# A second-stage DFT table without its zeros, spread onto zeroed memory, in a new sequence

## The chip, the cores and the metric

The kernel runs on one core of a Trainium2 chip. The metric is the device time of one execution in microseconds (us). The engines are called TensorE (PE in the profile, PEld its weight loads), VectorE (DVE), ScalarE (ACT), GpSimd (POOL) and SyncE (SP, which issues most DMAs).

## The reference

There are four residual layers on x of shape [2048, 512]: A, B, A, B. Layer A is an H3-style mixer: k is convolved with four taps for each channel, multiplied by v, convolved over the whole sequence with a kernel of length 2048 for each channel (through an FFT of length 4096), and gated with the normalised x. Layer B is an MLP of width 1376.

```python
def _A_ref(q, k, v, shift_k, ssm_k, ssm_D):
    ...
    for t in range(ks):                       # ks = 4
        k_shift = k_shift + k_pad[:, t:t + S, :] * shift_k[:, ks - 1 - t][None, None, :]
    kv = k_shift * v
    ...
    y_f = kv_f * kf_f[None, :, :, :]          # rfft of kv and of ssm_k, both padded to 2S
    y = irfft(y_f)[:S]                        # shortened here
    y = y + kv * ssm_D[None, None, :]
    return q * y

def _B_ref(x, w1, b1, w2, b2):
    y = _layernorm(x, axis=-1)
    h = _gelu(jnp.einsum("bsd,df->bsf", y, w1) + b1)
    return jnp.einsum("bsf,fd->bsd", h, w2) + b2

x = A_q
x = x + _A_ref(_layernorm(x, axis=-1), A_k, A_v, A_shift_k, A_ssm_k, A_ssm_D)
x = x + _B_ref(_layernorm(x, axis=-1), B_w1, B_b1, B_w2, B_b2)
x = x + _A_ref(...)                           # the same k, v and taps again
x = x + _B_ref(...)
```

The convolution is the same in both A layers, since k, v and the kernel are the same; the kernel computes it once.

## The kernel before

The whole program is recorded as 1114 operations (`P.op`), each with the engines that may run it, the memory it reads and writes, and its PSUM tile. Nothing is planned at run time: the tuple `ORDER` lists the operations' numbers in the order in which they are handed to their engines, `SECOND` names those that go to the second of two allowed engines, and `BANKS` gives each PSUM tile its bank. Every engine runs its own operations strictly in that order, and waits on semaphores where an operation needs another engine's result (`sync`). DMAs are operations of SP's queue (a few of ScalarE's).

The FFT is done as matrix products with tables. The names in the code (line numbers of the profile):

- `ht` (L528, evacuated at L453): TensorE transposes ssm_k with the identity, in four tiles of 16 matmuls; the identity comes from `tab_small` by ScalarE's first DMA.
- `h1` (L545): the first stage of the kernel's transform, 16 tiles of 16 matmuls with 64 weight columns.
- `h2` (L558, `stage2`): its second stage, 128 matmuls, one for each of 128 frequencies, in 16 tiles of eight; the weight of each is a 128x128 block of the table S2, which lies in `R_S2`. Then 16 DMAs (ar<-ar, 512-byte runs) make a copy with swapped partitions.
- `fir`: the four-tap filter, for two channel groups on VectorE (L450, 128x2048) and for two on TensorE (L589 transposes, L606 products, L613 multiplication by v). GpSimd makes the diagonal matrices for it (L520).
- `x1` (L545) and `x2` (L651, `products`): the two stages for kv; the second again takes the 128 blocks of S2 as weights, for 64 columns at a time, 256 matmuls in 16 tiles of 16. An evacuation by ScalarE or VectorE (L453) is followed by a VectorE multiplication with the kernel's spectrum (L450).
- `i1` (L674) and `i2` (L731): the inverse, 256 matmuls of 128 columns and 64 of 256 columns; the weights of `i1` are read at a step of four elements.
- Then, block by block of rows (`BLOCKS0`, `BLOCKS1`): statistics (L754, L756, L760, L762), norm (L768), gate and add (L450), a transposition (TensorE at L814 for the first two rows of blocks, DMA at L807 for the others), the first product `m1` (L827), gelu on ScalarE (L832), the second product `m2` (L860; L849 for the last), and the residual addition (L864, L853).

S2 holds, for each frequency, a 128x128 matrix that couples 32 rows and 32 columns for one of four channels d, so that three quarters of it are zeros: a row (r, a, d) meets only columns with the same d. Before, the whole table of 128 x 16384 bf16 lies in DRAM and is loaded by 16 DMAs of 1024 columns (L447), which in SP's queue stand between the loads of v. The loads of k, v and the table are recorded by `load(step)` in the order of `LOADS`; that gives them their numbers (before: 10 to 19 for k, 20 to 27 for v, 28 to 43 for the table).

One operation is number 4 in both kernels: `P.op(ACT, lambda e: e.preload_act_table(AF.Gelu_apprx_tanh))` (L465). It has no input, no output and no successor.

Of the kernel before, what the change touches and what calls it, by code (L numbers as in the profile page):

```python
# [38 lines left out]
class Prog:  # L39
# [6 lines left out]
        49, 0, 47, 8, 7, 1, 3, 6, 48, 14, 71, 68, 5, 72, 18, 17, 15, 12, 4, 69, 9, 70, 50, 16, 65, 13, 19, 94, 2, 53, 73, 96, 51, 52, 11,  # L46
        92, 66, 305, 62, 95, 100, 97, 67, 104, 93, 63, 28, 64, 90, 88, 105, 10, 101, 26, 44, 45, 84, 91, 24, 56, 78, 85, 79, 86, 33, 59, 76,
        89, 57, 87, 198, 77, 36, 102, 168, 60, 103, 35, 25, 98, 30, 27, 31, 82, 74, 310, 182, 54, 169, 80, 61, 29, 183, 58, 199, 99, 37, 22,
        154, 75, 46, 81, 83, 172, 184, 42, 32, 155, 43, 120, 110, 116, 173, 121, 111, 34, 55, 112, 113, 39, 124, 158, 200, 125, 185, 20,
        106, 201, 108, 117, 23, 114, 107, 21, 38, 41, 159, 118, 109, 128, 156, 115, 136, 119, 122, 202, 40, 186, 203, 129, 157, 141, 204,  # L50
        132, 137, 133, 123, 134, 166, 170, 167, 187, 205, 130, 162, 171, 306, 144, 135, 126, 131, 127, 164, 138, 174, 163, 206, 175, 165,
        176, 207, 178, 139, 180, 140, 212, 179, 181, 160, 177, 188, 142, 213, 210, 295, 146, 208, 153, 209, 161, 189, 150, 211, 214, 148,
        223, 215, 224, 217, 147, 218, 151, 220, 192, 196, 193, 145, 194, 221, 149, 190, 197, 195, 235, 143, 225, 219, 226, 191, 236, 297,
        222, 304, 152, 229, 232, 230, 298, 296, 257, 216, 299, 227, 254, 237, 231, 233, 263, 228, 258, 264, 260, 234, 255, 269, 275, 259,
        252, 261, 303, 270, 253, 242, 294, 250, 243, 256, 265, 276, 262, 271, 246, 266, 272, 376, 277, 267, 300, 268, 248, 273, 274, 247,
        238, 249, 239, 333, 421, 240, 377, 334, 244, 251, 284, 241, 245, 477, 285, 311, 335, 288, 479, 289, 278, 313, 419, 336, 337, 314,
        338, 279, 378, 420, 286, 379, 287, 292, 380, 422, 290, 280, 339, 531, 293, 282, 342, 423, 478, 291, 529, 315, 281, 424, 283, 425,
        480, 302, 581, 316, 307, 381, 321, 323, 430, 331, 324, 325, 317, 322, 481, 329, 382, 340, 301, 326, 383, 341, 332, 308, 431, 482,
        343, 384, 426, 344, 385, 345, 386, 530, 346, 387, 347, 319, 388, 318, 432, 389, 330, 428, 348, 483, 349, 320, 390, 327, 354, 427,
        532, 391, 438, 328, 392, 368, 352, 533, 356, 309, 350, 355, 429, 364, 435, 433, 409, 360, 486, 357, 351, 358, 434, 353, 365, 436,  # L60
        439, 437, 362, 484, 363, 440, 485, 393, 487, 361, 394, 441, 397, 372, 410, 582, 395, 398, 366, 401, 489, 403, 442, 370, 359, 396,
        402, 534, 404, 367, 413, 407, 399, 443, 445, 538, 405, 411, 373, 583, 488, 635, 406, 400, 408, 312, 535, 491, 369, 490, 584, 371,
        492, 444, 414, 633, 415, 374, 416, 493, 446, 634, 494, 636, 497, 585, 586, 453, 536, 412, 454, 495, 590, 539, 451, 459, 637, 638,
        537, 465, 447, 591, 455, 466, 375, 461, 452, 540, 739, 449, 587, 642, 541, 592, 457, 498, 460, 450, 417, 448, 463, 496, 588, 643,
        543, 418, 462, 464, 507, 458, 509, 456, 542, 737, 685, 467, 589, 639, 503, 505, 499, 506, 544, 504, 515, 508, 469, 640, 468, 510,
        470, 593, 513, 687, 511, 473, 517, 545, 686, 738, 644, 740, 519, 546, 688, 689, 512, 549, 471, 550, 501, 690, 595, 516, 594, 596,
        547, 597, 502, 474, 514, 789, 548, 500, 641, 791, 598, 691, 694, 475, 525, 692, 521, 695, 551, 561, 518, 520, 567, 522, 476, 693,
        526, 599, 555, 645, 553, 696, 741, 742, 601, 552, 565, 527, 795, 554, 472, 646, 563, 566, 602, 743, 697, 562, 569, 557, 793, 746,
        571, 647, 699, 790, 600, 523, 568, 558, 570, 556, 524, 621, 648, 649, 572, 792, 744, 794, 559, 796, 698, 603, 560, 747, 611, 564,
        650, 651, 573, 609, 797, 607, 612, 700, 701, 748, 745, 605, 606, 652, 798, 653, 619, 528, 869, 608, 623, 620, 577, 615, 617, 802,  # L70
        702, 624, 799, 800, 613, 803, 574, 801, 749, 705, 654, 610, 706, 618, 614, 808, 751, 578, 703, 673, 669, 604, 575, 670, 576, 665,
        579, 622, 659, 667, 657, 750, 811, 616, 666, 809, 625, 871, 626, 661, 674, 675, 873, 870, 752, 872, 580, 753, 804, 660, 810, 662,
        754, 875, 874, 629, 876, 704, 805, 711, 658, 676, 806, 655, 725, 712, 663, 627, 812, 630, 817, 877, 878, 631, 709, 656, 668, 757,
        628, 888, 726, 671, 672, 758, 889, 813, 715, 681, 807, 716, 815, 885, 719, 755, 949, 723, 879, 664, 717, 724, 707, 632, 882, 682,
        886, 677, 756, 720, 816, 713, 883, 814, 880, 818, 881, 819, 683, 773, 951, 890, 678, 710, 820, 823, 684, 825, 827, 721, 950, 727,
        887, 759, 679, 884, 891, 892, 714, 761, 708, 824, 729, 821, 826, 718, 897, 762, 774, 769, 767, 680, 952, 728, 763, 895, 760, 896,
        953, 771, 779, 722, 730, 898, 775, 955, 822, 893, 770, 954, 765, 894, 956, 957, 733, 768, 958, 962, 828, 780, 777, 965, 899, 900,
        901, 731, 905, 734, 766, 968, 735, 764, 903, 839, 966, 963, 902, 785, 907, 831, 840, 776, 964, 732, 959, 906, 969, 781, 736, 960,
        778, 772, 845, 782, 973, 904, 908, 835, 843, 786, 787, 841, 1031, 967, 788, 929, 1029, 913, 846, 961, 970, 783, 784, 975, 1033,
        1035, 842, 844, 1030, 930, 836, 925, 976, 1032, 971, 911, 1034, 829, 849, 1036, 1037, 1038, 915, 912, 909, 972, 830, 923, 1045, 977,  # L80
        833, 832, 919, 974, 1046, 926, 978, 847, 979, 914, 1048, 834, 920, 1039, 980, 850, 1049, 1042, 1047, 985, 910, 916, 837, 917, 855,
        1040, 1041, 838, 851, 1043, 986, 1050, 987, 981, 864, 860, 918, 848, 927, 856, 1051, 921, 1044, 1052, 1055, 1056, 983, 1057, 984,
        1053, 940, 922, 924, 865, 852, 857, 982, 988, 853, 858, 944, 995, 1058, 928, 1054, 861, 991, 854, 1059, 862, 997, 1003, 1060, 945,
        992, 931, 946, 1061, 866, 941, 998, 1004, 1063, 1001, 1009, 1064, 932, 947, 942, 1062, 996, 1067, 1068, 943, 1065, 867, 935, 1005,
        1010, 1066, 1007, 936, 1002, 993, 1008, 1069, 999, 994, 989, 1000, 1085, 990, 933, 1081, 937, 1073, 1082, 1083, 1086, 948, 1020,
        1006, 1070, 1075, 1071, 938, 863, 1077, 1076, 1074, 1089, 1024, 934, 1087, 1072, 1100, 1084, 1078, 859, 1079, 1091, 1080, 1011,
        1095, 1090, 1101, 1088, 1015, 1111, 1012, 1016, 1021, 1102, 1017, 1092, 1025, 1103, 1112, 939, 1013, 1026, 1022, 1113, 1014, 1093,
        1027, 1096, 1097, 1094, 1104, 1105, 868, 1023, 1018, 1098, 1028, 1019, 1108, 1106, 1099, 1109, 1107, 1110)
    SECOND = (
        63, 64, 66, 67, 69, 72, 89, 97, 105, 127, 155, 161, 169, 175, 177, 215, 221, 239, 291, 349, 392)  # L90
    BANKS = (
        0, 4, 2, 2, 0, 2, 2, 0, 6, 6, 0, 0, 4, 2, 4, 4, 0, 6, 4, 0, 2, 6, 2, 0, 6, 0, 4, 4, 2, 0, 2, 2, 4, 6, 0, 6, 4, 4, 4, 0, 6, 0, 2, 0,
        0, 6, 6, 2, 6, 4, 0, 6, 4, 0, 2, 6, 2, 6, 4, 2, 0, 2, 4, 6, 6, 2, 4, 0, 6, 2, 4, 4, 2, 4, 0, 2, 2, 0, 4, 6, 4, 0, 6, 6, 6, 6, 0, 0,
        0, 2, 4, 2, 4, 2, 2, 0, 6, 0, 0, 2, 6, 4, 4, 1, 5, 4, 0, 4, 3, 0, 6, 2, 7, 0, 6, 6, 1, 1, 5, 3, 5, 3, 4, 5, 2, 2, 1, 3, 7, 2, 2, 1,
        5, 4, 0, 1, 2, 1, 2, 5, 1, 6, 2, 4, 5, 1, 7, 2, 7, 0, 4, 3, 7, 6, 2, 4, 1, 0, 1, 0, 4, 2, 3, 2, 5, 1, 7, 5, 7, 2, 4, 7, 6, 3, 2, 3,
        0, 6, 1, 0, 6, 4, 0, 5, 5, 5, 2, 2, 1, 6, 6, 0, 2, 6, 7, 5, 4, 4, 5, 4, 7, 1, 4, 2, 6, 5, 3, 4, 2, 4, 1, 4, 3, 1, 7, 0, 0, 6, 4, 5,
        1, 3, 5, 3, 2, 7, 0, 3, 0, 2, 3, 7, 1, 6, 7, 7, 4, 6, 2, 1, 2, 5, 0, 0, 2, 0, 5, 4, 5, 6, 0, 6, 7, 3, 2, 2, 2, 7, 4, 3, 5, 0, 3, 4,
        4, 7, 2, 4, 1, 1, 6, 6, 3, 0, 2, 6, 1, 7, 6, 0, 2)

# [268 lines left out]
def bass_interleave_layers__ssm_conv_h3__mixer_channel_mlp__prompt_kernel(  # L368
# [115 lines left out]

    for step in LOADS:
        load(step)
# [414 lines left out]
```

## Time and profile before

| what | value |
|---|---|
| median of 3 runs | 242.24 us (241.83 to 243.01) |
| profiled execution | 240.63 us, span 238.8 us |
| busy: TensorE, VectorE, ScalarE, GpSimd | 226.2, 171.6, 138.3, 41.3 us |
| DMA | 27.40 MB in 37035 packets |
| granted TensorE clock | 1.00 |
| loads of S2 | 16 of 256 KB, median 9.6 us from issue to landing |

The span runs from the first to the last instruction of the program; the 1.8 us beside it are the start and end of the execution. A line of the profile names the source line, the engine, the operation with output and input, and how many instructions are merged in it. Operations recorded through a helper all carry the helper's line: L450 is every multiplication or addition of two tensors, L453 every evacuation, L439 and L447 the DMAs. A busy TensorE is not TensorE at its peak, since matmuls are pipelined and the profile models their ends; the pace of a run of matmuls (its length over their number) says more than the mean duration of one.

### The profile page before, as it was taken

What the parts mean: (1) busy time and instruction counts of PE and PEld (TensorE: products, weight loads), DVE (VectorE), ACT (ScalarE), POOL (GpSimd) and SP (SyncE); (2) the same over time, 40 slices, a digit from 0 to 9 for tenths busy, and PEclk for the clock granted to TensorE, in tenths of its full rate; (3) what the DMA queues carried; (4) which work ended last, traced back from release to release, by engine and by line L of the source; (5) the groups of instructions that cost most, each with busy time, mean ns of one, the idle gap of its engine ahead of it and who ended that gap; (6) DMA issues with size and microseconds to landing.
All of it is one profiled execution on the core that took longest, in us unless ns stands there. A gap on an engine that the chain in (4) does not pass through costs nothing.

```text
span 238.8 us, 5555 instructions
## 1 busy us (share of the span) xinstructions
PE 226.2 (95%) x2312; PEld 151.6 (63%) x2332; DVE 171.6 (72%) x359; ACT 138.3 (58%) x225; POOL 41.3 (17%) x77
## 2 busy tenths in 40 slices
PE   7987989886999999999999999999999999999995
PEld 3875778875899886766766667644444444444543
DVE  0979999999999999999887999693793312030035
ACT  2598799999999995642754444342782042454100
POOL 2179000000013444041230310400220200000000
PEclk9999999999999999999999999999999999999999
DMA  6999949999960003111122022240013021310024
GB/s 241 364 342 383 383 148 253 249 272 309 379 227 0 3 0 68 26 23 31 37 47 44 0 48 44 45 88 3 0 22 66 3 44 31 101 44 3 0 71 148
DMA packets 37035, 27.40 MB, mean 115 GB/s; under 512 B 19506, under 2 KB 29969, under 8 KB 37010
## 3 DMA queue, kind: packets, MB, share of 16 engines
q1 hardware_dynamic: 36446, 26.91, 37.8%
q8 instruction: 18, 0.29, 0.5%
q10 hardware_dynamic: 564, 0.14, 0.4%
q14 instruction: 7, 0.06, 0.1%
HBM read 16.82 MB, written 2.10 MB: 79 GB/s over the span
## 4 chain that ended last, share of the span: by engine, by line
PE 77%; ACT 9%; DMA 4%; DVE 4%; SPq 3%; issue 3%; ACTq 0%
PE ps L860 31%; PE ps L827 30%; ACT ar L453 9%; PE ps L674 5%; PE ps L731 3%; SPq L439 3%; PE ps L545 3%; DMA ar<-in_A_ssm_k_dram 2%; DVE ar L453 2%; DMA ar<-ar 2%; PE ps L528 1%; PE ps L606 1%; PE ps L849 1%; DVE sm L754 1%; PE ps L589 1%
## 5 line engine op out<-in xcount | busy, mean ns | idle before, releaser
L832 ACT ACTIVATE ar<-ps,sm 128x256 bf16<-128x256 f32 (+4 forms) x143 | 64.7, 525 | 72.5 <-PE ps L827 68.1
L827 PE MATMUL ps<-ar 128*128 128x256 bf16 (+4 forms) x568 | 84.2, 297 | 0.2
L860 PE MATMUL ps<-ar 128*128 128x512 bf16 (+1 forms) x329 | 79.0, 379 | 0.6
L453 ACT ACTIVATE ar<-ps 128x1024 bf16<-128x1024 f32 (+1 forms) x81 | 72.5, 1057 | 9.0 <-PE ps L511 4.5
L827 PEld LDWEIGHTS ps<-ar 128*128 128x128 bf16 (+1 forms) x572 | 52.9, 100 | 29.8 <-ACT ar L832 0.5
L450 DVE TENSOR_TENSOR ar<-ar 128x512 bf16<-128x512 bf16 (+3 forms) x106 | 63.6, 634 | 2.0 <-DMA ar<-in_A_k_dram 1.3
L860 PEld LDWEIGHTS ps<-ar 128*128 128x128 bf16 (+1 forms) x341 | 33.1, 98 | 34.3 <-ACT ar L832 0.3
L864 DVE TENSOR_TENSOR ar<-ar,ps 128x512 bf16<-128x512 bf16 x31 | 20.6, 680 | 47.3 <-PE ps L860 47.3
L754 DVE BATCH_NORM_STATS2 sm<-ar 128x6 f32<-128x512 bf16 (+1 forms) x68 | 42.8, 647 | 0.1
L768 DVE TENSOR_SCALAR ar<-ar,sm 128x512 bf16<-128x512 bf16 x64 | 25.0, 407 | 7.8 <-POOL sm L762 5.2
L760 POOL TENSOR_SCALAR sm<-sm 128x2 f32<-128x2 f32 (+2 forms) x26 | 6.0, 232 | 93.9 <-DVE sm L756 93.3
L762 POOL TENSOR_TENSOR sm<-sm 128x2 f32<-128x2 f32 (+2 forms) x26 | 21.6, 832 | 2.2
L545 PE MATMUL ps<-ar 128*64 128x128 bf16 x512 | 17.1, 221 | 1.4 <-issue 0.8
L545 PEld LDWEIGHTS ps<-ar 128*64 128x64 bf16 x512 | 14.9, 110 | 3.2 <-issue 1.0
L674 PE MATMUL ps<-ar 128*128 128x128 bf16 x256 | 15.0, 220 | 0.6 <-ACT ar L453 0.6
L674 PEld LDWEIGHTS ps<-ar 128*128 128x128 bf16 x256 | 14.7, 114 | 0.8 <-ACT ar L453 0.8
L453 DVE CAST ar<-ps 128x1024 bf16<-128x1024 f32 x11 | 13.0, 1212 | 0.3 <-PE ps L558 0.3
L651 PE MATMUL ps<-ar 128*128 128x64 bf16 x256 | 9.8, 194 | 3.2 <-ACT ar L453 2.7
L453 DVE COPY ar<-ps 128x2048 bf16<-128x2048 bf16 (+1 forms) x8 | 8.2, 1024 | 6.4 <-PE ps L528 6.3
L651 PEld LDWEIGHTS ps<-ar 128*128 128x128 bf16 x256 | 8.2, 98 | 4.7 <-ACT ar L453 3.9
L756 DVE BATCH_NORM_AGGREGATE sm<-sm 128x2 f32<-128x6 f32 (+1 forms) x64 | 9.9, 171 | 0.3
L558 PE MATMUL ps<-ar 128*128 128x128 bf16 x128 | 8.6, 220 | 0.8 <-ACT ar L453 0.8
(34 smaller groups left out, 78.1 us busy)
## 6 DMA issues: line engine op xcount, KB each, us to landing
ar<-tab_s SPq DMA_DIRECT2D x16, 256.0 KB, 9.6
ar<-ar SPq DMA_DIRECT2D x16, 256.0 KB, 4.2
ar<-in_A_ssm_k_dram SPq DMA_DIRECT2D x4, 512.0 KB, 5.3
ar<-in_A_k_dram SPq DMA_DIRECT2D x8, 256.0 KB, 7.6
ar<-in_A_v_dram SPq DMA_DIRECT2D x8, 256.0 KB, 9.6
ar<-in_A_q_dram SPq DMA_DIRECT2D x4, 512.0 KB, 7.9
out_dram<-ar SPq DMA_DIRECT2D x7, 256.0 KB, 2.1
ar<-in_B_w_dram SPq DMA_DIRECT2D x1, 1376.0 KB, 12.6
```

The costliest lines, as they stand in the source:

```text
L450: return P.op(eng, lambda e: e.tensor_tensor(o, a, b, op), reads=[a, b] + list(more), writes=[o])
L453: f = {ACT: lambda e: e.activation(dst, src(), AF.Copy), DVE: lambda e: e.tensor_copy(dst, src())}
L545: r = e.matmul(Q(tl, 64 * ri, 64, i * 128, [1, 128]), w, m, start=True, stop=True)
L651: r = e.matmul(Q(tl, 0, 128, i * pitch, [1, n]), w, m, start=True, stop=True)
L674: r = e.matmul(Q(tl, 0, 128, i * 128, [1, 128]), w, m, start=q == 0, stop=q == 1)
L754: P.op(DVE, lambda e, sj=sj, x=x: e.bn_stats(sj, x), reads=[x], writes=[sj])
L762: P.op(POOL, lambda e: e.tensor_tensor(r, v, hf, ALU.pow), reads=[v, hf], writes=[r])
L768: P.op(DVE, lambda e: e.tensor_scalar(o, x, m, r, ALU.subtract, ALU.mult), reads=[x, m, r], writes=[o])
L827: r = e.matmul(Q(tl, 0, rows, 0, [1, w]), a, m, start=dk == 0, stop=dk == 3)
L832: P.op(ACT, lambda e, dst=dst, tl=tl, rows=rows, bias=bias, w=w: e.activation(dst, Q(tl, 0, rows, 0, [1, w]), AF.Gelu_apprx_tanh, bias=bia ...
L860: r = e.matmul(Q(tl, 0, 128, 0, [1, 512]), ins[fc][0], ins[fc][1], start=fc == 0, stop=fc == 10)
L864: P.op(DVE, lambda e, x=x, tl=tl: e.tensor_tensor(x, x, Q(tl, 0, 128, 0, [1, 512]), ALU.add), reads=[x], writes=[x], tile=tl)
```

## The change

The table keeps one channel's 32 x 32 block for each frequency, 32 x 4096 bf16 in DRAM, arranged in groups of four frequencies (`SG`), in which a column's four values lie side by side. Eight memsets (on GpSimd or VectorE, as float32) clear `R_S2`. Eight DMAs, four for each half of the frequencies and one for each d, write the table to every fourth partition in runs of 128 elements (256 bytes); all four read the same source. The two halves are now the first two steps of `LOADS`. Weights of `h2` and `x2` are read at a step of four elements (`[SG, 128]`). The output columns of the second stage are in the order (d, k2, real or imaginary) instead of (k2, d, ...), and the rows of the table U follow.

The number of operations is the same (16 loads become 8 memsets and 8 loads), but these and the loads of k and v get other numbers (10 to 17 the memsets, 18 to 25 the table, 26 to 35 k, 36 to 43 v). `ORDER`, `SECOND` and `BANKS` are new throughout. What they make of some operations: in VectorE's queue four memsets stand ahead of everything, one behind its first `ht` evacuation and one behind the third; two stand in GpSimd's queue behind its first two. The first table load stands in SP's queue behind the four loads of ssm_k and the eight of k, and waits for the memset behind VectorE's first evacuation; the others stand between v's loads. On ScalarE's queue the load of the identity comes third among its four DMAs instead of first. Operation 4 stands between operations 830 and 976 instead of between 12 and 69.

```diff
     ORDER = (
-        49, 0, 47, 8, 7, 1, 3, 6, 48, 14, 71, 68, 5, 72, 18, 17, 15, 12, 4, 69, 9, 70, 50, 16, 65, 13, 19, 94, 2, 53, 73, 96, 51, 52, 11,
...
+        1, 49, 47, 6, 10, 11, 3, 17, 48, 0, 12, 16, 8, 5, 65, 15, 66, 50, 67, 2, 71, 13, 7, 62, 72, 51, 88, 52, 53, 63, 89, 32, 45, 73, 9,
...
+        830, 4, 976, 978, 916, 913, 848, 843, 919, 1048, 910, 833, 839, 836, 834, 927, 922, 1043, 972, 1040, 860, 840, 1044, 1055, 928, 844,
...
     SECOND = (
-        63, 64, 66, 67, 69, 72, 89, 97, 105, 127, 155, 161, 169, 175, 177, 215, 221, 239, 291, 349, 392)
+        10, 11, 13, 14, 15, 17, 63, 66, 67, 69, 72, 81, 83, 93, 125, 161, 169, 175, 177, 191, 221, 224, 251, 283, 349, 392)
...
-    S2 = S2.transpose(0, 1, 2, 3, 5, 6, 4).reshape(128, 128 * 128)
+    S2 = S2[:, :, 0, :, :, :, 0].transpose(0, 1, 2, 4, 3).reshape(32, 128 // SG, SG, 32)
+    S2 = S2.transpose(0, 1, 3, 2).reshape(32, 4096)
...
-    U = U.transpose(1, 2, 0, 3, 4, 5, 6).reshape(128, 256)
+    U = U.transpose(2, 1, 0, 3, 4, 5, 6).reshape(128, 256)
...
-LOADS = ("k", "v") + tuple(range(16))
+LOADS = (0, 1, "k", "v")
+SG = 4
...
-            tload(t_s2, 128 * 128, step * 1024, R_S2 + step * 1024, 1024)
-
+            for d in range(4):
+                dst = bass.AP(ar, d * AR + R_S2 + 32 * SG * d + 8192 * step, [[4 * AR, 32], [128 * SG, 64 // SG], [1, 32 * SG]])
+                src = bass.AP(t_s2, 2048 * step, [[4096, 32], [32 * SG, 64 // SG], [1, 32 * SG]])
+                P.op(SP, lambda e, dst=dst, src=src: e.dma_start(dst.bitcast(U16), src), writes=[dst], dma=True)
+
+    for i in range(8):
+        z = A(0, 128, R_S2 + 2048 * i, [1, 2048])
+        P.op((POOL, DVE), lambda e, z=z: e.memset(z.bitcast(F32), 0.0), writes=[z])
...
-        ins = [(i, A(0, 128, R_S2 + k * 128, [1, 128]), A(0, 128, G + k * n, [1, n])) for i, k in enumerate(ks)]
+        ins = [(i, A(0, 128, R_S2 + k // SG * 128 * SG + k % SG, [SG, 128]), A(0, 128, G + k * n, [1, n])) for i, k in enumerate(ks)]
...
-            ins = [(i, A(0, 128, R_S2 + (k0 + i) * 128, [1, 128]), A(0, 128, R_GX + 128 * d0 + (k0 + i) * n, [1, n]))
+            ins = [(i, A(0, 128, R_S2 + (k0 + i) // SG * 128 * SG + (k0 + i) % SG, [SG, 128]), A(0, 128, R_GX + 128 * d0 + (k0 + i) * n, [1, n]))
```

## The prediction

> **What bounds the kernel now.** I read the page's engine shares and chain first, then the busy time by stretches of the span, then the timeline at the places where one engine hands over to another.
>
> ```profile
> PE 77%; ACT 9%; DMA 4%; DVE 4%; SPq 3%; issue 3%; ACTq 0%
> ...
> 48.00:64.00 16.00, 12.87 (x310) 11.29 (x306) 16.00 (x15) 16.00 (x19) 0.21 (x1) 1.00 1.00 313
> 64.00:84.00 20.00, 19.72 (x292) 18.42 (x293) 19.38 (x52) 19.70 (x24) 5.83 (x16) 1.00 0.27 102
> 84.00:236.00 152.00, 151.16 (x919) 87.35 (x933) 96.11 (x258) 65.28 (x144) 23.04 (x41) 1.00 0.17 37
> ```
>
> (Columns after the stretch: its length, then PE, weight loads, VectorE, ScalarE, GpSimd busy; granted clock, DMA share, GB/s.) The MLP is TensorE's: its moving columns are 2 layers x 2048 rows x 44 for each of the two products, in units of 512 columns 704 matmuls; 22 of them took 4.76 us at 183.6 us (0.216 each), so 152.2 us, and the stretch from the first MLP matmul (83.1) to the last (236.4) is 153.3. Some 1 us of waiting is all that can be saved there. Before 64 us VectorE and ScalarE are full and TensorE waits. The DMA share is 1.0 there too, but no engine waits for a table in the list of waits. The timeline says which engine ends each part:
>
> ```profile
> 2.07 1.28 ACT L465 ACT_TABLE_LOAD   x1 [2.07 <-issue]
> ...
> 16.42 2.36 DVE L450 TENSOR_TENSOR ar<-ar 128x2048 bf16<-128x2048 bf16 x2 [1.28 <-DMA ar<-in_A_k_dram]
> ...
> 64.13 0.68 DVE L754 BATCH_NORM_STATS2 sm<-ar 128x6 f32<-128x512 bf16 x1
> 64.73 3.48 DVE L450 TENSOR_TENSOR ar<-ar 128x2048 bf16<-128x2048 bf16 x3
> 64.92 6.56 PE L674 MATMUL ps<-ar 128*128 128x128 bf16 x112 [0.28 <-ACT ar L453]
> ...
> 78.17 6.58 ACT L453 ACTIVATE ar<-ps 128x512 bf16<-128x512 f32 x8 [0.21 <-PE ps L731]
> 83.59 2.74 PE L827 MATMUL ps<-ar 128*128 128x128 bf16 x44
> 84.56 4.22 ACT L832 ACTIVATE ar<-ps,sm 128x128 bf16<-128x128 f32 x15
> ```
>
> VectorE runs from 16.42 to 68.2 (64.73 + 3.48) with two waits of 0.33, and the last product multiplication ends there. TensorE, at 0.0586 us a matmul in the inverse first stage (6.56 / 112), needs 64 more for the first half and would start the second half, which wants that multiplication, at 64.92 + 3.75 = 68.67. The two are level. From there TensorE never stops, and ScalarE goes straight from the last evacuation to the first gelu at 84.56.
>
> **The change, part by part.** Durations are those of the profiled execution (240.63 us, span 238.8), 1.6 below the median 242.24; I add differences to both alike.
>
> *Table traffic.* 16 loads of 256 KB in 2 KB runs become 8 of 128 KB in 4096 runs of 256 bytes. At 24 to 30 us, 383 GB/s at full DMA share make 86 ns a 2 KB run on one of 16 engines: 2048 runs cost 11.0 us of all of them. Runs of 512 bytes (the copies ar<-ar, 254 GB/s at 36 to 42 us) make 32 ns. A 256-byte run lies between 24 (the straight line through both) and 32: 6.1 to 8.2 us. Some 3 to 5 us of DMA time go, and 8 SP issues of 0.49 against 0.66 (the row of the 512-run copies). Worth on the path: nothing, as no wait on a table is in the trace; the cover is the stage of the kernel spectrum before it. Arrival: k's loads close the first 4 MB, which at 370 GB/s from 2 us are through at 12.8, and landed at 16.4, so landings trail by 3.6. The table's first half closes 6 MB: 18.2 + 3.6 = 21.8, up to 24.5 with 32 ns for its 2048 runs; TensorE wants it at 24.6, as before. The second half: 2 + 16.2 for 6 MB + 6.1 to 8.2 + 3.6 = 27.9 to 30, wanted at about 30 (the seventh tile of that stage ran at 29.7, and VectorE, which it follows, is later now). Behind a late table TensorE stands in order, with VectorE's FIR products behind it.
> The page DMA: Bandwidth & Descriptors of the Trainium skill (Specifications) speaks against this part: it states 512 bytes as the smallest transfer at line rate, with read-modify-write below. By that, a 256-byte run would cost a 512-byte one or more; no transfer of this trace shows plain 256-byte copies.
>
> *SP's wait.* The first table load stands behind the eight k loads and waits for a memset that VectorE runs after its first copy, till about 8.8 us; SP gets there at 6.7. Queued behind it are all v loads and the k halos. The 4 MB issued by then last the DMA engines past 12 us at 366 GB/s, so nothing arrives late enough to be noticed: 0.
>
> *Memsets.* Eight of 128x1024 f32. No row shows that; POOL took 0.53 us for 512 elements (1.03 ns each), so 1.06, with 0.53 as the lower end. Two on POOL and four on VectorE lie in the first 5 us, when both are idle: 0. Two on VectorE stand among the first evacuations. There the queue held 8.9 us of work from 6.04 (2.54 + 0.35 + 1.23 + 1.21 + 1.23 + 2.35); it now holds one small add more (0.18) and the two memsets. It also starts later: on ScalarE's queue the identity is issued third, at 1.6 instead of 0.74, and with its landing time of 3.5 TensorE starts at 5.2 instead of 4.78. So 6.5 + 8.9 + 0.2 + 2.1 = 17.7 instead of 16.42 (16.6 at the lower end); k's landing, about 16.4, no longer binds. **+1.2** at VectorE (+0.2, to +1.6 if the identity lands 0.4 later still).
>
> *The searched order, up to 68 us.* VectorE gives one transposed-k evacuation to ScalarE (-1.2) and takes one of the first-stage evacuations (+1.2); one BATCH_NORM_STATS2 (0.68) moves behind the last product, and the two waits of 0.33 may go. 68.2 + 1.2 - 0.68 - (0 to 0.67) = 68.1 to 68.7, against TensorE's own 68.67. **0** (-0.5 to +0.4). ScalarE has one evacuation less (-0.94), and the one it gains falls into its 2.58 wait for the second stage.
>
> *Weights at a step of four.* Rows with a step of four (L674), one (L651) and sixteen (L528):
>
> ```profile
> L674 PEld LDWEIGHTS ps<-ar 128*128 128x128 bf16 x256 | 14.7, 114 | 0.8 <-ACT ar L453 0.8
> L651 PEld LDWEIGHTS ps<-ar 128*128 128x128 bf16 x256 | 8.2, 98 | 4.7 <-ACT ar L453 3.9 <-DVE ar L453 0.7
> L528 PEld LDWEIGHTS ps<-ar 128*128 128x128 bf16 x64 | 4.4, 150 | 1.3 <-DMA ar<-in_A_ssm_k_dram 0.7 <-DVE ar L453 0.4
> ```
>
> L674 reads at a step of four already and holds the pace of contiguous weights with 128 columns (57 ns), so the 128 matmuls of the kernel spectrum lose nothing. The 256 product matmuls have 64 columns and run at 32 ns (64 in 2.03 us); with stepped weights 32 to 57, and by L674's 16 ns over L651 (L528 has 52 over it, and holds 68 a matmul) about 48, so a tile of 16 takes 0.78 instead of 0.52. It hides under VectorE's 1.16 a tile: 0, up to +1.5 if TensorE becomes the bound there.
>
> *A second and a third table load on ScalarE.* This is the part that no line of the diff names: operation 4, the preload of the gelu table, stood 19th in ORDER and now stands between 830 and 976, in the last layer. So ScalarE's first copies have another table loaded for them (in its idle time before 6 us: 0), the gelu table is loaded in front of the first gelu, and the preload loads it again late. The last has cover: ScalarE is busy 65 of 152 us there. The middle one has none: ScalarE comes late from the last evacuation (84.75, 1.6 after TensorE's last tile), and TensorE runs ahead only as far as banks allow, eight MLP tiles of 0.22; then it needs the first gelu, and the first second product needs the fifth. Cost 1.28 by the row, less what TensorE has in hand (0.1 to 0.6): **+1.2**.
> The page ScalarE: Activation LUTs of the Trainium skill (What ACT_TABLE_LOAD costs) gives 1283 ns for the load, which this trace shows to the digit, and 1380 ns more for emptying the pipeline, which no row here shows; by it the sum would be 1.4 higher, which is the case of the dearer load below.
>
> *The rest of the order.* Counting TensorE's work before each block's first MLP matmul and VectorE's before its norm, both shift the same way (block 5: +2.1 and +2.0 us; the first of the second layer +3.2 and +3.1), so no block lacks its input. 0 (-0.5 to +1.0).
>
> Sum: 0 + 1.2 + 0.1 for the weights: 241.9 for a profiled execution, 243.5 as a median.
>
> **The rivals.**
> *Faster.* The two memsets cost their lower end and the waits of 0.33 go, so the products end 1.3 early (68.2 + 0.2 - 0.68 - 0.67 = 67.05), and ScalarE, an evacuation lighter, has caught up at 84 us, so that the table load finds it idle. For it: 0.94 less on ScalarE. Against: TensorE's own 68.67 must come earlier as well, through ScalarE. It decides where ScalarE ends the last evacuation within 0.3 us of TensorE. -1.4: 240.8.
> *Nothing on the path.* The load is hidden as above, the front is level: 242.2, 241.6 to 242.9. The same comes out if the smaller table does all it says, since its traffic was hidden.
> *The load is dearer than its row.* If the load waits for the end of the copy before it (copies of 1024 columns last 1.06 and follow each other at 0.94), 0.1 is added; at twice the row, 2.56, the sum is 1.3 higher: 244.8. For it: the one row stood in an empty queue. The page ScalarE: Activation LUTs of the Trainium skill points here.
> *The tables come late.* If a 256-byte run costs 48 ns, half as much again as the 512-byte row, 4096 take 12.3 us and the second half lands at 34; TensorE stands before its seventh tile of the kernel spectrum from 30, and VectorE, whose FIR product behind that tile is next at 33, gets it at about 36.4: 3.4 lost, 246.9 (245 to 250). Against: a row of 512 bytes holds 32. It decides from a landing past 32 us. The rule on 512 bytes in DMA: Bandwidth & Descriptors of the Trainium skill points here.
>
> **How the numbers follow.** My forecast 0.44, its own range 242.9 to 244.9; the dearer load 0.06; late tables 0.18; nothing 0.14; faster 0.18. A measurement of this kernel tells about 0.5%, 1.2 us, from no change: 241.0 to 243.5. Of the forecast 0.26 lies above and 0.18 inside, of the faster case 0.01 inside; so faster 0.17, same 0.18 + 0.14 + 0.01 = 0.33, slower 0.26 + 0.06 + 0.18 = 0.50. The range 240.6 to 246.6 leaves out half of the faster case (0.09) and rather over half of the late tables (0.10).
>
> **What would show it.** An ACT_TABLE_LOAD of 1.28 between ScalarE's last copy and first gelu, with TensorE idle about 1.2 in the first MLP block; the first product on k at 17 to 18 us; two memsets of about 1.06 among VectorE's first copies; the weight loads of the product line between 98 and 114; no wait on tab_s. A wait of TensorE for a table, or a first gelu level with the last copy, would prove me wrong.

## The result, and the profile after

The changed kernel takes 245.03 us (median of 6 runs, 243.69 to 246.03), the kernel before in the same comparison 241.96 (240.85 to 243.01). The ratio is 1.0134, 95% interval 1.0088 to 1.018: slower by 3.1 us. The profiled execution took 245.01 us with a span of 243.2, against 240.63 and 238.8. Ratios and medians leave out the runs that are more than 1.5% above the fastest of their kernel (one of E5's, two of E7's, three of E9's six below), ranges hold all runs, and a ratio is not the quotient of two medians, so the two can differ by a few tenths of a per cent.

The shares of the engines in the chain that ended last, from the page of the kernel after:

```profile
PE 75%; ACT 20%; DMA 2%; issue 1%; ACTq 0%; DVE 0%
```

ScalarE has 20% of the chain instead of 9%, and VectorE has gone from it. The busy time by stretches reads as before, with the boundaries moved by the lateness; one of them (columns as in the prediction, where it is the stretch from 64 to 84):

```profile
64.00:88.00 24.00, 23.52 (x363) 22.19 (x359) 23.25 (x56) 23.87 (x29) 6.15 (x15) 1.00 0.43 163
```

The work has only moved to the right. Two places made it move. First the start, in the timeline of TensorE and of VectorE (start, length, and in brackets the idle time before and what ended it):

```profile
1.56 3.60 PE L507 MATMUL ps<-ar 128*128 128x512 bf16 x8 [1.56 <-POOL ar L501]
6.33 1.93 PE L536 MATMUL ps<-ar 128*128 128x128 bf16 x16 [1.17 <-DMA ar<-tab_small]
...
9.15 3.64 PE L536 MATMUL ps<-ar 128*128 128x128 bf16 x32
12.71 1.84 PE L553 MATMUL ps<-ar 128*64 128x128 bf16 x32
14.49 1.23 PE L536 MATMUL ps<-ar 128*128 128x128 bf16 x16
...
9.68 0.91 DVE L492 MEMSET ar<- 128x1024 f32 x1 [0.16 <-issue]
...
20.55 2.34 DVE L452 TENSOR_TENSOR ar<-ar 128x2048 bf16<-128x2048 bf16 x2
...
66.57 4.63 DVE L452 TENSOR_TENSOR ar<-ar 128x2048 bf16<-128x2048 bf16 x4 [0.40 <-issue]
67.05 9.30 PE L682 MATMUL ps<-ar 128*128 128x128 bf16 x160 [0.19 <-ACT ar L455]
```

The eight warm-up matmuls end at 5.16; the identity (`tab_small`) lands 1.17 us later. Then 32 transposes take 3.64 us, and the 32 matmuls of the first stage behind them (L553) 1.84, where E3 below does them in 1.08; the last sixteen transposes, from 14.49, take 1.23. So the slow pace lasts until about 14.3 us. In the kernel before TensorE is quick from the end of its warm-up on, whose last two matmuls take 0.79 us instead of 1.06. Its timeline:

```profile
4.78 2.52 PE L528 MATMUL ps<-ar 128*128 128x128 bf16 x32
```

So the first product on k comes at 20.55 instead of 16.42, and the last product multiplication ends at 66.57 + 4.63 = 71.2 instead of 68.2. The last tile of the inverse second stage ends at 86.24 instead of 83.25: 3.0 us are lost up to there. The second place is the hand-over to the MLP. In the kernel before, the last inverse tile and the first second product:

```profile
82.21 1.04 PE L731 MATMUL ps<-ar 128*128 128x256 bf16 x8
...
86.38 0.81 PE L860 MATMUL ps<-ar 128*128 128x512 bf16 x3
```

The same place in the kernel after:

```profile
85.20 1.04 PE L739 MATMUL ps<-ar 128*128 128x256 bf16 x8
...
87.51 1.28 ACT L840 ACT_TABLE_LOAD   x1
88.81 2.69 ACT L840 ACTIVATE ar<-ps,sm 128x128 bf16<-128x128 f32 x10
89.23 0.94 PE L835 MATMUL ps<-ar 128*128 128x128 bf16 x12 [1.06 <-ACT ar L840]
...
90.31 1.03 PE L868 MATMUL ps<-ar 128*128 128x512 bf16 x4
```

The gelu table is loaded between ScalarE's last evacuation and its first gelu, and TensorE stands 1.06 us for it. The first second product is at 90.31 instead of 86.38: 3.93 late, of which 0.94 is new here. The rest of the span is 243.2 - 90.31 = 152.9 against 152.4. So 3.0 + 0.9 + 0.5 = 4.4, the difference of the two spans. The profiled execution of the kernel before (240.63) lies under all its timed runs of this comparison, which is why the profiles differ by more than the medians.

No instruction waits for `tab_s`. The weight loads of the products, from the costliest groups (busy us and mean ns of one, then the idle time before):

```profile
L659 PEld LDWEIGHTS ps<-ar 128*128 128x128 bf16 x256 | 9.6, 118 | 2.4 <-ACT ar L455 2.0
```

The product line, now at a step of four, loads in 118 ns instead of 98; L682, which had the step already, keeps its 114.

### The profile page after: what moved, and what is told of

Read it like the earlier page. It is cut to its first block, busy times and chain, and to the rows that moved or that the text cites. A ratio compares the mean times of both kernels' runs of the same rounds, so it can differ in the third digit from the quotient of the medians.

```text
span 243.2 us, 5572 instructions
## 1 busy us (share of the span) xinstructions
PE 232.4 (96%) x2332; PEld 155.9 (64%) x2332; DVE 177.0 (73%) x366; ACT 141.6 (58%) x227; POOL 37.7 (15%) x78
## 3 DMA queue, kind: packets, MB, share of 16 engines
q1 hardware_dynamic: 38366, 23.77, 34.2%
## 4 chain that ended last, share of the span: by engine, by line
PE 75%; ACT 20%; DMA 2%; issue 1%; ACTq 0%; DVE 0%
PE ps L835 31%; PE ps L868 30%; ACT ar L455 20%; PE ps L682 5%; PE ps L536 3%; DMA ar<-tab_small 2%; PE ps L614 1%; PE ps L553 1%; PE ps L857 1%; PE ps L566 1%; ACT L840 1%; PE ps L519 0%; ACTq L441 0%; PE ps L659 0%; PE ps L739 0%
## 5 line engine op out<-in xcount | busy, mean ns | idle before, releaser
L835 PE MATMUL ps<-ar 128*128 128x256 bf16 (+4 forms) x572 | 83.2, 298 | 1.1 <-ACT ar L840 1.1
L868 PE MATMUL ps<-ar 128*128 128x512 bf16 (+1 forms) x341 | 80.1, 380 | 0.0
L452 DVE TENSOR_TENSOR ar<-ar 128x512 bf16<-128x512 bf16 (+3 forms) x107 | 64.4, 626 | 0.9 <-issue 0.4
L770 POOL TENSOR_TENSOR sm<-sm 128x2 f32<-128x2 f32 (+2 forms) x26 | 20.1, 773 | 2.2
L553 PE MATMUL ps<-ar 128*64 128x128 bf16 x512 | 18.7, 227 | 1.6 <-ACT ar L455 1.0
L553 PEld LDWEIGHTS ps<-ar 128*64 128x64 bf16 x512 | 15.7, 114 | 3.7 <-ACT ar L455 2.3
L682 PE MATMUL ps<-ar 128*128 128x128 bf16 x256 | 15.2, 220 | 0.8 <-ACT ar L455 0.8
L682 PEld LDWEIGHTS ps<-ar 128*128 128x128 bf16 x256 | 14.6, 114 | 1.1 <-ACT ar L455 1.1
L455 DVE CAST ar<-ps 128x1024 bf16<-128x1024 f32 x12 | 14.3, 1210 | 0.0
L659 PE MATMUL ps<-ar 128*128 128x64 bf16 x256 | 10.8, 199 | 1.3 <-ACT ar L455 1.1
L455 DVE COPY ar<-ps 128x2048 bf16<-128x2048 bf16 (+1 forms) x7 | 7.0, 994 | 6.2 <-PE ps L536 4.5
L659 PEld LDWEIGHTS ps<-ar 128*128 128x128 bf16 x256 | 9.6, 118 | 2.4 <-ACT ar L455 2.0
```

The lines of the kernel that those rows point to most:

```text
L452: return P.op(eng, lambda e: e.tensor_tensor(o, a, b, op), reads=[a, b] + list(more), writes=[o])
L455: f = {ACT: lambda e: e.activation(dst, src(), AF.Copy), DVE: lambda e: e.tensor_copy(dst, src())}
L553: r = e.matmul(Q(tl, 64 * ri, 64, i * 128, [1, 128]), w, m, start=True, stop=True)
L659: r = e.matmul(Q(tl, 0, 128, i * pitch, [1, n]), w, m, start=True, stop=True)
L682: r = e.matmul(Q(tl, 0, 128, i * 128, [1, 128]), w, m, start=q == 0, stop=q == 1)
L770: P.op(POOL, lambda e: e.tensor_tensor(r, v, hf, ALU.pow), reads=[v, hf], writes=[r])
```

## The theories

Theory 1: the identity's lateness leaves TensorE idle behind its warm-up, and it is the slow pace after that idle time, not the 1.2 us themselves, that costs the front its 3 us; the table load costs the rest. Theory 2, the prediction's own step: VectorE's queue is what is late, through the two memsets among its first evacuations. Each experiment ran 12 times (E9 six times) with the kernel before beside it on the same chip; "against before" is the difference of the two medians of that comparison. Line numbers differ by a few from kernel to kernel.

## E1 to E3: identity first, preload early, both

E1 puts the load of the identity back at the head of ScalarE's queue, E2 the preload back in the front, E3 does both:

```diff
-        1, 49, 47, 6, 10, 11, 3, 17, 48, 0, 12, 16, 8, 5, 65, 15, 66, 50, 67, 2, ...
+        0, 1, 49, 47, 6, 10, 11, 3, 17, 48, 12, 16, 8, 5, 65, 15, 66, 50, 67, 4, 2, ...
-        830, 4, 976, ...
+        830, 976, ...
```

> The kernel after, with the load of the identity issued first on ScalarE's queue again (operation 0 at the head of ORDER), nothing else changed. Theory 1 (the late identity): in the kernel after, TensorE ended its warm-up matmuls at 5.16 us, stood 1.17 us for the identity, and then ran sixteen matmuls of 128 columns in 1.68 us until 14.4 us, where the kernel before ran them in 1.08; this put the first product on k from 16.42 to 20.55 and the last product multiplication from 68.2 to 71.2. With the identity first, TensorE starts at 4.8, the sixteen take about 1.1 from the start, the first product on k is at 17 to 18, the last product ends at 68.2 to 69, and the time falls by 2 to 3: 242 to 243 as a median. Theory 2 (the two memsets in VectorE's queue, and SP's wait, delay the front; the identity is only a symptom): TensorE starts earlier but VectorE's first product on k stays at 20 or later, and the time falls by 0 to 0.5: 244.5 to 245.

> The kernel after, with the preload of the gelu table (operation 4) back in its early place in ORDER, nothing else changed, so that ScalarE has one table load instead of three. If the middle load costs what the trace shows between the last evacuation and the first gelu, the first gelu comes 1.1 to 1.3 us earlier against the last tile of the inverse stage and the time falls by as much: 243.7 to 243.9 as a median; the front (first product on k at 20.5, last product ended at 71.2) stays. Rival: TensorE finds work for the time of the load, or ScalarE is late for another reason, and the time falls by under 0.5.

> The kernel after, with the identity first and the preload early. Theory 1 with the load: the two gains add, 3.2 to 4.2 us, so 240.8 to 241.8 as a median, level with the kernel before (241.96) or a little under it: table, runs of 256 bytes, weights at a step of four, memsets and the rest of the searched order are then worth about nothing together. Theory 2: about 243.5, by the table load alone, and the rest of the loss stays with the memsets.

| kernel | median (range) | against before | ratio (95%) |
|---|---|---|---|
| after | 245.03 (243.69 to 246.03) | +3.07 | 1.0134 (1.0088 to 1.018) |
| E1 | 242.13 (241.42 to 242.78) | +0.55 | 1.0009 (0.9983 to 1.0034) |
| E2 | 243.47 (242.02 to 244.68) | +1.89 | 1.0061 (1.0025 to 1.0098) |
| E3 | 241.06 (240.32 to 241.61) | -0.52 | 0.9956 (0.9925 to 0.9986) |

One moved DMA gives back 2.5 us (3.07 - 0.55; 1.89 + 0.52 = 2.4 with the preload early), and the preload 1.1 to 1.2. The two add up, and with both mended the change is a little faster than the kernel before. The late load of the identity is what costs the front; how much of that is the slow pace and how much the lateness itself, E4 tells. The timeline of E3, TensorE and VectorE:

```profile
1.56 3.60 PE L509 MATMUL ps<-ar 128*128 128x512 bf16 x8 [1.56 <-POOL ar L503]
4.99 1.93 PE L538 MATMUL ps<-ar 128*128 128x128 bf16 x16
...
7.47 2.23 PE L538 MATMUL ps<-ar 128*128 128x128 bf16 x32
9.63 1.08 PE L555 MATMUL ps<-ar 128*64 128x128 bf16 x32
...
8.35 0.91 DVE L494 MEMSET ar<- 128x1024 f32 x1
...
17.56 2.34 DVE L454 TENSOR_TENSOR ar<-ar 128x2048 bf16<-128x2048 bf16 x2
```

There is no idle time behind the warm-up. The first sixteen transposes are still slow, but from about 7.1 us the pace is quick (32 transposes in 2.23). The first product on k is at 17.56, and VectorE had no wait from 8.35 to there. The load itself can be read from the hand-over: from the end of the last inverse tile to the first second product it takes 83.66 to 86.32, 2.66 us in E3, and 83.99 to 88.06, 4.07, in E1. So the middle load costs 1.41 there. E2 (2.65) agrees with E3, and the kernel after (4.07) with E1.

E2 shows a second form of the slow start. Its TensorE was idle for 1.43 us, ran sixteen transposes in 1.23 and then went slow, until 11.8 us. This time the granted clock says so (columns: length, TensorE busy, granted clock, DMA share, GB/s):

```profile
7.00:8.00 1.00, 1.00 (x15) 1.00 0.98 351
...
9.00:10.00 1.00, 1.00 (x12) 0.50 0.97 322
...
12.00:13.00 1.00, 1.00 (x35) 1.00 1.04 381
```

The clock is 0.68 in the microsecond before these 0.50 and 0.61 in the last before 12: some 3.4 us at half of it. Against what was expected, E2's front did not stay: the first product on k came at 19.10 in this profile, not at 20.5. Six of its twelve runs, this one among them, those with a mean granted clock of 0.992 or 0.993, took 242.0 to 243.3; the others 243.7 to 244.7.

## E4 and E9: the late identity with more warm-up, and the early one with less

E4 is the kernel after with more warm-up, E9 the kernel before with less:

```diff
-        for i in range(8):      # E4, in the kernel after
+        for i in range(13):
-        for i in range(8):      # E9, in the kernel before
+        for i in range(4):
```

> The kernel after, with 13 warm-up matmuls instead of 8, so that TensorE has work until the identity lands at about 6.3 us; the identity stays third. Theory 1a (it is the idle 1.17 us that leaves TensorE at the slow pace): the first transposes start at 6.3 to 7 still, but sixteen matmuls take about 1.1 us from the start or soon after, the first product on k is at 18.5 to 19, and the time falls by 1.5 to 2.5. Theory 1b (the lateness of the identity by itself, or something else that makes TensorE slow until 14.4 us): the sixteen stay at 1.68, and the time is 0 to 0.5 longer.

> The kernel before, with 4 warm-up matmuls instead of 8 and the identity first as ever, so that only the idle time is made, without a later identity: the warm-up ends at about 3.4 us and the identity lands at 4.8 to 5. If the idle stretch ahead of the transposes is what leaves TensorE at the slow pace, the first 32 transposes take 3.6 us instead of 2.5, the quick pace begins at 8 us or later instead of 5, the first product on k is at 17.5 or later, and the time is 1 to 3 us over the kernel before: 242.4 to 244.4. If it needs a late identity, the transposes start at 4.8 to 5 at the quick pace and the time stays within 0.4: 241.0 to 241.8.

E4: 243.43 (242.97 to 243.94), +1.85 against before, ratio 1.0071 (1.0045 to 1.0096), where the kernel after has +3.07. E9: 244.99 (242.9 to 247.62; the median is of three runs), +3.3, ratio 1.0181 (1.0131 to 1.023). First the timeline of E4, then that of E9, which is from its fastest run (242.9):

```profile
1.56 4.75 PE L507 MATMUL ps<-ar 128*128 128x512 bf16 x13 [1.56 <-POOL ar L501]
7.29 1.21 PE L536 MATMUL ps<-ar 128*128 128x128 bf16 x16 [0.98 <-DMA ar<-tab_small]
...
8.97 2.21 PE L536 MATMUL ps<-ar 128*128 128x128 bf16 x32
```

```profile
1.56 1.89 PE L499 MATMUL ps<-ar 128*128 128x512 bf16 x4 [1.56 <-POOL ar L493]
5.08 3.64 PE L528 MATMUL ps<-ar 128*128 128x128 bf16 x32 [1.62 <-DMA ar<-in_A_ssm_k_dram]
...
19.93 1.22 DVE L453 COPY ar<-ps 128x2048 bf16<-128x2048 bf16 x1 [1.02 <-PE ps L589]
```

In E4 the transposes start a microsecond later than in the kernel after (7.29 against 6.33) and TensorE still stands idle for 0.98 before them, yet TensorE is quick at once, and the time is better by 1.2, a little less than expected (1.5 to 2.5). It had stepped up during the longer warm-up: thirteen matmuls take 4.75 us, where eight took 3.60. Against E3, whose identity is early, E4's transposes start 2.3 us later at the quick pace, its last product ends 1.2 later (69.73 against 68.51), and the medians are 2.4 apart, of which the table load is 1.1 to 1.4. So the lateness by itself costs about 1 us too, and theory 1, which put the whole loss on the slow pace, holds for about half of it or somewhat more.

In E9 next to nothing is late (the transposes start at 5.08 instead of 4.78), but the warm-up is short: TensorE is idle 1.62 and the 32 transposes take 3.64 us, as in the kernel after. The first product on k is at 16.55, not at 17.5 or later as expected; the loss comes behind it. TensorE reaches the transposes of the filter (L589) at 18.82 instead of 17.00, VectorE waits 1.02 us for them, and the last product ends at 69.64 instead of 68.2. Taking away warm-up alone thus makes the slow pace and a later end of the front, and giving more undoes 1.2 of the 3.1. E9's median lies above the range expected (242.4 to 244.4); what its slower runs lose beyond the profiled one is not in a trace, and stays open.

In the profiles TensorE steps up 3.1 to 8.0 us after it began to work without a break of 1 us, at a point that differs from run to run. The kernel before steps at about 4.6 (3.1 after 1.56), E4 at 5.4 (3.8 after), E3 at 7.1 (5.5 after), E9 at 8.9 (3.8 after 5.08), E5 at 10.9 (4.2 after 6.66), the kernel after at 14.3 (8.0 after 6.33); the other profiles lie between. E2 was quick right behind its break and lost the pace from 8.3 us, for 3.4 us. Eight warm-up matmuls of 0.45 us last 3.6 us, about the least of these times. The page TensorE: Matmul & The Clock Gate of the Trainium skill (What's actually happening) states that the clock doubles after one window of 3.4 us in which TensorE was busy, that an idle window halves it, and that the windows run freely. By that figure the step would come one to two windows after work starts, an estimate of 3.4 to 6.8 us. E3, E4, E5 and E9 agree; the kernel before is just under it and the kernel after beyond it, and in E2 the clock fell behind an idle stretch of 1.43 us, not of a whole window. Here the traces decide: a far shorter break than a window was enough, and why the kernel after took 8.0 us is open. No row shows the windows themselves.

## E5 and E6: the two faults put into the kernel before

E5 moves only the load of the identity behind the two small ones on ScalarE's queue, E6 only the preload:

```diff
-        49, 0, 47, 8, 7, 1, 3, 6, 48, ...      # E5, ORDER of the kernel before
+        49, 47, 8, 7, 1, 3, 0, 6, 48, ...
-        12, 4, 69, ...                         # E6
+        12, 69, ...
-        976, ...
+        4, 976, ...
```

> The kernel before, with one step moved: the load of the identity third on ScalarE's queue, as in the kernel after (operation 0 behind operation 3). If the late identity by itself does it (theory 1), TensorE stands over 1 us after its eight warm-up matmuls and then runs at the slow pace (sixteen matmuls of 128 columns in 1.7 to 1.9 us) for 3 to 8 us more, the first product on k goes from 16.4 to 18.5 or later, and the time is 2 to 4 us over the kernel before: 243.6 to 245.6. If only the lateness counts, as the prediction had it, TensorE starts 0.4 to 1.5 us later at the quick pace and the time is 0 to 0.6 over: 241.6 to 242.2.

> The kernel before, with one step moved: the preload of the gelu table (operation 4) in the last layer, as in the kernel after, so that ScalarE loads three tables instead of one. By the prediction's step it costs the 1.28 us of the load before the first gelu, less 0.1 to 0.6 that TensorE has in hand: +1.0 to +1.2, 242.6 to 242.8, with the front as before. The kernel after less its load (244.99 against 243.47) and with the identity first (242.13 against 241.06) gave 1.1 to 1.6. Rival: the dearer load, +2.5.

E5: 243.89 (242.51 to 247.56), +2.5, ratio 1.0101 (1.0064 to 1.0139). Its timeline shows the idle time and the slow pace again:

```profile
6.66 3.63 PE L530 MATMUL ps<-ar 128*128 128x128 bf16 x32 [1.50 <-DMA ar<-tab_small]
```

The first product on k then came at 18.35. One DMA behind two small ones costs the old kernel as much as it cost the new one, with no memset and no table in play.

E6: 242.82 (242.24 to 243.62), +1.47 by the medians, ratio 1.0026 (0.9993 to 1.0058), which alone would not settle it. The timeline of E6 does:

```profile
85.49 1.28 ACT L834 ACT_TABLE_LOAD   x1
...
87.20 1.17 PE L829 MATMUL ps<-ar 128*128 128x128 bf16 x16 [1.06 <-ACT ar L834]
```

From the last inverse tile (83.96) to the first second product (88.24) it takes 4.28 us, against 3.13 in the kernel before: 1.15 for the load. The first gelu starts as the load ends (85.49 + 1.28 = 86.77, first gelu 86.78), so the dearer load is refuted. The old order's hand-over without the load took 2.91 in the profiles of E5 and E7, so 1.15 is the lower end: by these it is 1.37.

## E7: the table alone

E7 has the new table, memsets and weights, and for the rest the order of the kernel before, with all memsets in the front, four on GpSimd and four on VectorE:

```diff
+        49, 0, 47, 10, 11, 12, 13, 14, 15, 16, 17, 8, 7, 1, 3, 6, 48, ...
```

> The change of the table alone: eight table loads of 128 KB spread in runs of 256 bytes onto zeros set in the front, weights of the product at a step of four, and for the rest the order of the kernel before (identity first, preload early, BANKS and SECOND of before; four memsets on GpSimd, four on VectorE while it has no work). By the prediction's steps for the table, the wait on SP and the weights (0, 0, 0.1) it is level with the kernel before: 241.2 to 242.2, no wait on tab_s, product tiles of 0.7 against 0.6 us. Rival (runs of 256 bytes come late, or the stepped weights make TensorE the bound): 243 or more, with a wait of TensorE for tab_s or VectorE waiting for product tiles.

242.21 (241.08 to 245.76), +0.9 by the medians, ratio 1.000 (0.9963 to 1.0038); the profiled run took 241.29 with a span of 239.5. No wait for `tab_s`. Timeline of E7:

```profile
17.35 2.38 DVE L454 TENSOR_TENSOR ar<-ar 128x2048 bf16<-128x2048 bf16 x2 [1.87 <-DMA ar<-in_A_k_dram]
...
64.01 0.72 PE L661 MATMUL ps<-ar 128*128 128x64 bf16 x16 [0.20 <-ACT ar L457]
64.91 3.48 DVE L454 TENSOR_TENSOR ar<-ar 128x2048 bf16<-128x2048 bf16 x3
```

A product tile takes 0.72 instead of 0.64 and VectorE's multiplications follow without a gap, so the stepped weights are covered. By the ratio the table by itself is not told apart from nothing. The median is at the upper end of the expected range, and the interval allows 0.9 either way; the first product on k waited 1.87 for k's landing, against 1.28 in the kernel before and 1.49 in E6, and whether the table's traffic made k later was not separated.

## E8 and E10: the memsets off VectorE's queue, and more warm-up

E8 is E3 with the two memsets taken from VectorE's queue and put on GpSimd ahead of the evacuations. E10 is E8 with 11 warm-up matmuls.

```diff
-        0, 1, 49, 47, 6, 10, 11, 3, 17, 48, 12, 16, 8, ...
+        0, 1, 49, 47, 6, 10, 11, 3, 17, 48, 12, 16, 14, 13, 8, ...
     SECOND = (
-        10, 11, 13, 14, 15, 17, ...
+        10, 11, 15, 17, ...
```

> The kernel of the third run (identity first, preload early) with the two memsets that stood among VectorE's first evacuations done by GpSimd ahead of them (operations 13 and 14 behind 16, out of SECOND). In that run VectorE had no wait from 8.35 to the first product on k at 17.56 us, and the two memsets are 2 x 1.07 of it. If VectorE sets the end of the front, the first product on k is at 16.4 to 16.6, the last product ends 1 us earlier, and the time falls by 0.5 to 1.0: 240.0 to 240.5. If k's landing or TensorE's inverse first stage (68.67 in the kernel before) binds next, it falls by under 0.3: 240.8 to 241.1.

> The kernel of the eighth run (identity first, preload early, memsets ahead on GpSimd: 240.49) with 11 warm-up matmuls instead of 8, to close what is left of the idle stretch before the identity. If that stretch still costs it something, the runs at 240.9 to 242.8 go and the median falls by 0.1 to 0.3: 240.2 to 240.4. If the three matmuls only hold the transposes up (0.22 to 0.45 us each), VectorE's first copy comes 0.3 to 0.8 later and the median rises by as much or, where VectorE's waits for TensorE take it up, by 0 to 0.3: 240.5 to 241.2.

E8: 240.49 (240.24 to 242.75), -0.86 against before, ratio 0.9966 (0.9937 to 0.9994). That is 0.3 lower than E3 by the medians and no lower by the ratio (0.9956), so the two are not told apart. The first product on k comes at 16.15 instead of 17.56, and the last product multiplication ends at 63.64 + 4.63 = 68.27, 0.24 earlier than in E3. Of the 1.41 at k, 0.47 is there before any of the memsets: in E8's profile TensorE is quick from the first transpose on, and VectorE's first copy starts at 6.49 instead of 6.96. So the memsets were on VectorE's path up to k, but little of it reached the end. E8 has the lowest median of all the runs, and its interval lies below the kernel before.

E10: 241.83 (241.06 to 243.54), +0.2, ratio 1.0003 (0.9975 to 1.0032): worse than E8 by about 1, and above what either case expected. The timeline of E10 shows the price of more warm-up; it is from the slowest of its runs, in which the granted clock also fell to 0.91 between 20 and 40 us:

```profile
1.56 4.88 PE L509 MATMUL ps<-ar 128*128 128x512 bf16 x11 [1.56 <-POOL ar L503]
6.23 1.26 PE L538 MATMUL ps<-ar 128*128 128x128 bf16 x16
```

The transposes are quick at once, but start at 6.23 instead of 5.24, and the first product on k slips to 17.18. Here the warm-up outlasted the input, and the first product on k came later by as much as the transposes did.

## Why the prediction came out as it did

The sign held. The difference was put at +1.3 us and is +3.1: the time, 245.03, lies inside the stated 240.6 to 246.6 and just above the forecast's own range, 242.9 to 244.9. Step by step:

- *Table traffic, 0.* Right: no wait for `tab_s` in any run, and the DMA share falls off after 26 us instead of 32. The run of 256 bytes was, if anything, priced too high. The main queue's packets took 34.2% of 243.2 us instead of 37.8% of 238.8, 7.1 us less on each of 16 engines, 4.5 less in E7 and 7.4 in E8. With the estimate of 11.0 for the loads removed, 4096 runs cost 3.5 to 6.5 us by one profile each, 14 to 25 ns a run against the 24 to 32 of the prediction. The rival of late tables is refuted here, and with it, for this traffic, the price at which the 512-byte rule of the page DMA: Bandwidth & Descriptors of the Trainium skill (Specifications) would have decided.
- *SP's wait, 0.* Nothing in the traces contradicts it. SP waits 3.8 us for the memset in the kernel after and 2.4 in E3. E8, which moves that memset to GpSimd, has no such wait and is not told apart from E3; the wait was not tried by itself.
- *Memsets and the first product on k, +1.2.* This is the step that failed, and only in one term: "TensorE starts at 5.2 instead of 4.78". The landing was put 3.5 us after the issue; it took 4.7 here, and TensorE started at 6.33. The worse fault is that a later start was priced as a shift of 0.4 at an unchanged pace. The idle time put the end of the slow pace some 9.5 us further, and the term is worth 2.4 to 2.5 us (E1, E3) and 2.5 in the kernel before (E5), of which lateness alone is about 1 (E4). In the sum the +1.2 had been set off against the searched order, so that the front stood at 0; it lost 3.0. The memsets were priced well: 0.91 and a pitch of 1.07 against 1.06, and with the identity mended the product on k is at 17.45 (E1) and 17.56 (E3) against the 17.7 predicted.
- *Searched order up to 68 us, 0 (-0.5 to +0.4).* Right once the start is mended: the last product ends at 68.51 in E3, +0.3.
- *Weights at a step of four, 0.1.* The load is 118 ns, slightly above the bounds of 98 to 114; sixteen loads take 0.61 us, 38 ns each against the 48 estimated. Covered, as predicted.
- *Table loads, +1.2.* Right: 1.1 to 1.2 by the medians of E1 to E3, +1.15 in E6's timeline, 1.41 in E3's hand-over against E1's. Against the kernel before only 0.94 of the 1.41 is lost at the hand-over, since without the load that of the new order is the shorter one (2.66 against 3.13). Why it is shorter is open: ScalarE does 74 evacuations of 1024 columns instead of 75, as the faster rival had seen, but also one of 2048 columns more, which takes 1.97 us in the kernel after. The first and the last load are covered, as said. The prediction's 1.6 from TensorE's last tile to the end of the last evacuation is 1.5 by its own rows (84.75 and 83.25), which changes nothing.
- *The rest of the order, 0 (-0.5 to +1.0).* From the first second product to the end 152.9 us against 152.4, in one profile each: +0.5.

So the forecast came near because one term was right. The other was wrong by a mechanism that the profile of before showed only in its eight warm-up matmuls (3.33 us, 0.42 each, where the prediction counts 0.216 for 512 columns later on); that its 3 us still fell inside 240.6 to 246.6 is luck, since the upper part of that range was there for late tables. The sign of the faster rival is true of the mended kernels: E3 and E8 beat the kernel before by 0.5 and 0.9. Why E3 does so is not settled: its profile is 0.5 us longer than that of the kernel before, which was itself below all six timed runs of its first comparison. That the first product on k no longer waits for a landing that varies (1.28, 1.49 and 1.87 us of wait in three profiles of the old order) would fit, but was only argued.

## What to carry to other kernels

Where TensorE starts on a warm-up, let the load that its first real work waits for land before the warm-up ends, or the warm-up last until TensorE has stepped up. Price a late load by the slow pace that follows as well as by the lateness: here 1.2 to 1.5 us of idle time cost 2.4 to 2.5. Follow every operation without a data dependence through a new order, since a table preload or a small DMA that slips behind others is named by no line that changes. And judge a change that comes with a new order by mending the order first: here the table by itself was not told apart from nothing, and two places of the new order lost 3.5 us; without them the changed kernel is 0.5 us faster than the kernel before.

## What was unexpected of the hardware

- The slow pace need not show in the granted clock. The kernel after shows 1.00 in every microsecond from 6 to 14 us, at about 110 ns a transpose (3.64 us for 32), where the quick pace is 70 (2.21 for 32 in E4); E2 shows 0.50 for the same pace. The pace of a run of equal matmuls is the safer row. The page TensorE: Matmul & The Clock Gate of the Trainium skill (Seeing it yourself) warns that the records of the clock are unreliable, and these rows agree.
- A break of 1.2 to 1.6 us right behind a warm-up of 1.9 to 3.6 us cost 2.4 us or more by the medians (the lateness that went with it included), while one of 0.98 behind a warm-up of 4.75 cost no pace at all (E4).
- A weight load at a step of four took 114 to 118 ns instead of 98, whether for 64 or 128 columns, and only the pace with 64 columns rose, 32 to 38 ns a matmul.
